# DeltaNet and low-rank mixer on one Trainium2 core: another order of the steps from the eighth chunk of the first recurrence on

## The chip, the cores and the metric

The kernel runs on one core of one Trainium2 chip. The metric is the device time of one execution in microseconds (us); of several executions the median is taken. Smaller is better.

## The reference

All data are float32. q, k and v have the shape (batch 4, heads 8, sequence 768, head size 48), beta (4, 8, 768). Two blocks follow each other:

```python
# 1. delta rule, for every batch and head a 48 x 48 state
k_n = k / (norm(k) + 1e-06)
for t in range(768):
    y[t] = q[t] @ state
    v_old = state.T @ k_n[t]
    state = state + beta[t] * outer(k_n[t], v[t] - v_old)
x = y.transpose(0, 2, 1, 3).reshape(4, 768, 384)      # heads side by side

# 2. low-rank mixer over the sequence, then a channel MLP
h = x.transpose(0, 2, 1) @ U @ V                       # U (768, 32), V (32, 768)
u = x + h.transpose(0, 2, 1)
out = u + relu(u @ w_ch1) @ w_ch2                      # (384, 1536), (1536, 384)
```

## The kernel before

**The recurrence in chunks.** A batch b is cut into two units, n = 2b and n = 2b + 1, each half of the sequence; a unit into six chunks of 64 tokens, so a batch has chunks 0 to 11. Within a chunk the tokens' dependence on one another is a triangular system, solved ahead of the recurrence; only the state of 48 x 48 goes from chunk to chunk. All eight heads are worked on together. The steps of a unit n, with their lines:

- load: q, k, v and beta come in by DMAs issued on SP and GpSimd.
- turn: k and q are transposed, in units 0 to 2 at least partly by TensorE (L681, copied out by ScalarE), in the others by VectorE (L756). i is 0 for k and 1 for q, j is the half of the heads.
- products: k k^T and q k^T of a chunk on TensorE (L709), copied out by ScalarE and VectorE (L740).
- norms: one operation on ScalarE and five on VectorE (L631 to L636), which give the scale of a token's key.
- blocks: VectorE lays the diagonal blocks for the substitution (L803), substitutes in many pairs of operations (L812, L818), and lays the result back (L825).
- joins, for half h of the chunks: small matmuls that put the blocks together (L869, L883, L909, L927), with copies on ScalarE and VectorE between them.
- prepare: two groups of matmuls that apply the solved system to k and v (L1032, L1043).

recur of batch b then goes chunk by chunk: state times key (TensorE, L1081), z = v minus that (VectorE, L1094), key times z (TensorE, L1109), new state (VectorE, L1120). outputs of chunk c multiplies q with the old state (L992) and adds the part within the chunk (L1006); ScalarE copies the result into X (L976). A TensorE group here has 16 matmuls.

**The mixer.** front of batch b and part i (256 tokens): for i = 0 the product with U (L1401), which VectorE copies (L1407); then the product with V (L1420), VectorE's addition (L1425), the transposes (L1444) and ScalarE's copy (L1447) into ut. channels e (0 to 5) is the first product of the MLP in two groups of six matmuls (L1505), with relu on ScalarE (L1470). add_up (L1532) and narrow e (L1625, gathered by VectorE at L1545) are the second product, written with seven products in place of eight for a 2 x 2 split. quick (L1305) is the first product of the last batch. load_weights turns the mixer's weights, which come in as 64-bit floats, into float32 on ScalarE (L1207) and VectorE (L1221, L1228, L1235), slice by slice; start i issues the DMAs of slice i (384 KB for most). reserve hands two of TensorE's result banks over to the MLP.

**Kinds of TensorE group.** L1401, L1444, L1505, L1625, L1305 and the turns use the array whole, or in column strips (L1401). The products, prepare, recur, outputs and L1420 use it as four quadrants of 64 x 64; the joins, as pieces of 32 x 32.

**What sets the order.** Every step above is a generator that yields one entry for each operation or small group it issues. The kernel waits for nothing at build time and plans nothing: a written table, ORDER, names for each of 2,259 positions the step that moves on by one. The order in which instructions are issued is the order in which each engine takes them from its queue; waits on other engines are put in as the data need them.

```python
ORDER = [x.rsplit(":", 1) for x in " ".join(ORDER.split()).split("; ")]
ORDER = {int(y): name for name, at in ORDER for y in at.split()}
...
def run():
    wake()
    for y in range(len(ORDER)):
        i = ORDER[y]
        s, got = waits[i], None
        ...
        advance(i, got, state["now"])
        wake()
```

An entry such as "outputs b0 c11: 467 473 478 480" says that the outputs of chunk 11 of batch 0 move on at those four positions (two TensorE groups, two ScalarE copies). Between the entries of one step those of other steps stand.

Of the kernel before, what the change touches and what calls it, by code (L numbers as in the profile page):

```python
# [27 lines left out]
def kernel(  # L28
# [116 lines left out]
    add_up b0 i0 f00: 615 655 660; add_up b0 i0 f03: 632 643 656; add_up b0 i1 f00: 794 798 818; add_up b0 i1  # L145
    f03: 826 827 829; add_up b0 i2 f00: 970 988 1025; add_up b0 i2 f03: 1018 1022 1032; add_up b1 i0 f00: 1164
    1193 1217; add_up b1 i0 f03: 1203 1206 1216; add_up b1 i1 f00: 1320 1332 1340; add_up b1 i1 f03: 1376 1382
    1395; add_up b1 i2 f00: 1522 1553 1593; add_up b1 i2 f03: 1566 1592 1596; add_up b2 i0 f00: 1678 1702 1728;
    add_up b2 i0 f03: 1718 1719 1727; add_up b2 i1 f00: 1873 1884 1890; add_up b2 i1 f03: 1878 1879 1893; add_up
    b2 i2 f00: 1994 2003 2018; add_up b2 i2 f03: 2038 2039 2044; add_up b3 i0 f00: 2177 2182 2183; add_up b3 i0  # L150
    f03: 2181 2184 2187; add_up b3 i1 f00: 2208 2209 2215; add_up b3 i1 f03: 2207 2214 2216; add_up b3 i2 f00:
    2225 2230 2241; add_up b3 i2 f03: 2226 2231 2232; blocks n0: 61 73 75 76 82 84 86 88 89 91 93 94 96 97 103
    110 114 122; blocks n1: 143 157 160 163 173 175 179 192 201 206 208 212 213 215 218 219 226 229; blocks n2:
    475 497 498 499 505 508 510 513 514 515 516 517 518 519 520 521 522 528; blocks n3: 687 699 700 704 716 727
    729 730 738 745 754 765 766 769 770 773 774 778 787 788 795 796 803 809 810 811 812 813 815 816 828 832 833
    835; blocks n4: 968 976 980 984 985 986 992 996 1002 1011 1026 1041 1053 1055 1057 1060 1062 1063 1075 1078
    1082 1104 1107 1109 1116 1117 1118 1119 1120 1121 1122 1130 1131 1132; blocks n5: 1161 1194 1226 1227 1228
    1231 1234 1239 1242 1243 1246 1254 1255 1257 1258 1266 1281 1285 1286 1289 1291 1300 1303 1310 1330 1333
    1334 1336 1337 1338 1339 1353 1365 1366; blocks n6: 1495 1507 1516 1518 1520 1521 1524 1526 1527 1528 1538
    1543 1544 1551 1555 1556 1580 1585 1590 1602 1603 1615 1616 1620 1640 1641 1646 1647 1653 1654 1665 1666  # L160
    1668 1669; blocks n7: 1673 1682 1683 1690 1691 1711 1745 1749 1750 1751 1760 1768 1769 1773 1776 1798 1804
    1805 1817 1818 1819 1820 1827 1828 1829 1830 1833 1834 1836 1837 1838 1839 1840 1844; both f0: 2127; both
    f1: 2097; both f2: 2163; both f3: 2123; both f4: 2151; both f5: 2179; channels b0 i0 e0: 523 524; channels
    b0 i0 e1: 525 531; channels b0 i0 e2: 532 543; channels b0 i0 e3: 553 555; channels b0 i0 e4: 573 574;
    channels b0 i0 e5: 595 624; channels b0 i1 e0: 748 760; channels b0 i1 e1: 761 764; channels b0 i1 e2: 771
    775; channels b0 i1 e3: 783 785; channels b0 i1 e4: 814 819; channels b0 i1 e5: 820 821; channels b0 i2 e0:
    898 899; channels b0 i2 e1: 907 908; channels b0 i2 e2: 932 933; channels b0 i2 e3: 957 966; channels b0 i2
    e4: 973 975; channels b0 i2 e5: 989 991; channels b1 i0 e0: 1114 1115; channels b1 i0 e1: 1125 1126;
    channels b1 i0 e2: 1128 1129; channels b1 i0 e3: 1138 1146; channels b1 i0 e4: 1153 1155; channels b1 i0 e5:
    1175 1181; channels b1 i1 e0: 1276 1277; channels b1 i1 e1: 1294 1295; channels b1 i1 e2: 1297 1298;  # L170
    channels b1 i1 e3: 1316 1321; channels b1 i1 e4: 1326 1356; channels b1 i1 e5: 1357 1359; channels b1 i2 e0:
    1449 1459; channels b1 i2 e1: 1477 1478; channels b1 i2 e2: 1499 1500; channels b1 i2 e3: 1509 1523;
    channels b1 i2 e4: 1529 1530; channels b1 i2 e5: 1540 1547; channels b2 i0 e0: 1642 1643; channels b2 i0 e1:
    1644 1645; channels b2 i0 e2: 1656 1657; channels b2 i0 e3: 1661 1663; channels b2 i0 e4: 1664 1679;
    channels b2 i0 e5: 1692 1693; channels b2 i1 e0: 1807 1809; channels b2 i1 e1: 1846 1847; channels b2 i1 e2:
    1849 1850; channels b2 i1 e3: 1852 1853; channels b2 i1 e4: 1857 1858; channels b2 i1 e5: 1862 1863;
    channels b2 i2 e0: 1946 1954; channels b2 i2 e1: 1957 1958; channels b2 i2 e2: 1959 1975; channels b2 i2 e3:
    1977 1987; channels b2 i2 e4: 1998 2008; channels b2 i2 e5: 2023 2032; copies f0: 2108 2116; copies f1: 2083
    2088; copies f2: 2144 2149; copies f3: 2091 2109; copies f4: 2102 2113; copies f5: 2147 2156; cut f0 k0 to0:
    2150; cut f0 k0 to1: 2148; cut f0 k1 to1: 2137; cut f1 k0 to0: 2138; cut f1 k0 to1: 2204; cut f1 k1 to1:  # L180
    2139; cut f2 k0 to0: 2166; cut f2 k0 to1: 2205; cut f2 k1 to1: 2203; cut f3 k0 to0: 2154; cut f3 k0 to1:
    2135; cut f3 k1 to1: 2172; cut f4 k0 to0: 2110; cut f4 k0 to1: 2188; cut f4 k1 to1: 2171; cut f5 k0 to0:
    2176; cut f5 k0 to1: 2202; cut f5 k1 to1: 2186; diagonals n0 h0: 188 190 191 195 210 222; diagonals n0 h1:
    167 169 171 176 181 186; diagonals n1 h0: 312 315 319 336 343 353; diagonals n1 h1: 290 292 303 338 349 358;
    diagonals n2 h0: 590 592 600 602 611 612; diagonals n2 h1: 649 650 678 680 681 691; diagonals n3 h0: 873 874
    875 878 895 897; diagonals n3 h1: 850 851 852 905 916 951; diagonals n4 h0: 1141 1142 1144 1145 1191 1209;
    diagonals n4 h1: 1170 1173 1184 1202 1207 1213; diagonals n5 h0: 1384 1390 1391 1420 1425 1428; diagonals n5
    h1: 1372 1378 1393 1407 1437 1438; diagonals n6 h0: 1695 1723 1734 1747 1765 1771; diagonals n6 h1: 1722
    1733 1735 1744 1753 1758; diagonals n7 h0: 1911 1912 1915 1919 1929 1940; diagonals n7 h1: 1891 1892 1935
    1936 1961 1963; first f0: 2132; first f1: 2101; first f2: 2157; first f3: 2125; first f4: 2104; first f5:  # L190
    2164; front b0 i0: 490 492 502 504 511 512; front b0 i1: 547 560 596 620; front b0 i2: 628 629 645 648;
    front b1 i0: 1061 1066 1070 1072 1096 1101; front b1 i1: 1113 1152 1250 1260; front b1 i2: 1307 1309 1410
    1431; front b2 i0: 1579 1589 1594 1614 1622 1630; front b2 i1: 1636 1726 1730 1777; front b2 i2: 1779 1783
    1854 1865; front b3 i0: 2035 2040 2042 2046 2048 2049; front b3 i1: 2057 2062 2063 2064; front b3 i2: 2067
    2070 2071 2072; gather b0 i0 h0 c0 finalFalse: 657; gather b0 i0 h0 c0 finalTrue: 668; gather b0 i0 h0 c1
    finalTrue: 740 918; gather b0 i0 h1 c0 finalFalse: 686; gather b0 i0 h1 c0 finalTrue: 741 884; gather b0 i0
    h1 c1 finalFalse: 693; gather b0 i0 h1 c1 finalTrue: 724; gather b0 i1 h0 c0 finalFalse: 830; gather b0 i1
    h0 c0 finalTrue: 834; gather b0 i1 h0 c1 finalTrue: 886 1133; gather b0 i1 h1 c0 finalFalse: 856; gather b0
    i1 h1 c0 finalTrue: 883 921; gather b0 i1 h1 c1 finalFalse: 868; gather b0 i1 h1 c1 finalTrue: 877; gather
    b0 i2 h0 c0 finalFalse: 1024; gather b0 i2 h0 c0 finalTrue: 1054; gather b0 i2 h0 c1 finalTrue: 1105 1178;  # L200
    gather b0 i2 h1 c0 finalFalse: 1071; gather b0 i2 h1 c0 finalTrue: 1110 1162; gather b0 i2 h1 c1 finalFalse:
    1068; gather b0 i2 h1 c1 finalTrue: 1079; gather b1 i0 h0 c0 finalFalse: 1204; gather b1 i0 h0 c0 finalTrue:
    1232; gather b1 i0 h0 c1 finalTrue: 1264 1871; gather b1 i0 h1 c0 finalFalse: 1244; gather b1 i0 h1 c0
    finalTrue: 1263 1504; gather b1 i0 h1 c1 finalFalse: 1248; gather b1 i0 h1 c1 finalTrue: 1249; gather b1 i1
    h0 c0 finalFalse: 1380; gather b1 i1 h0 c0 finalTrue: 1381; gather b1 i1 h0 c1 finalTrue: 1445 1739; gather
    b1 i1 h1 c0 finalFalse: 1400; gather b1 i1 h1 c0 finalTrue: 1436 1763; gather b1 i1 h1 c1 finalFalse: 1412;
    gather b1 i1 h1 c1 finalTrue: 1427; gather b1 i2 h0 c0 finalFalse: 1572; gather b1 i2 h0 c0 finalTrue: 1600;
    gather b1 i2 h0 c1 finalTrue: 1629 1785; gather b1 i2 h1 c0 finalFalse: 1607; gather b1 i2 h1 c0 finalTrue:
# [1495 lines left out]
```

## Time and profile before

| | before |
|---|---|
| median of 3 runs | 596.03 us (594.77 to 596.44) |
| the profiled execution's own time | 598.21 us |
| its span | 596.2 us |
| TensorE instructions | 10,428 matmuls, 10,428 weight loads |
| VectorE, ScalarE, GpSimd instructions | 1,011, 442, 229 |
| DMA, whole execution | 36.23 MB, mean 61 GB/s |
| mean granted TensorE clock | 0.943 |

The profile is of one execution, whose own time is 2.2 us above the median of the runs, and 2.0 us above its span. Engines are PE (TensorE matmuls), PEld (its weight loads, which overlap the matmuls), DVE (VectorE), ACT (ScalarE), POOL (GpSimd) and SP. "L1505" is line 1505 of the kernel. A view of stretches gives for each engine the busy us and, in brackets, the number of instructions, then the granted clock of TensorE as a share of full speed, the DMA engines' mean busy share and the rate. The chain of waits is followed back from the last instruction: each row is a start in us, a length, and what was running on it; "issue" is time in which an engine waited for nothing that the profile shows.

### The profile page before, as it was taken

The numbers are of one execution on the slowest core, as the hardware profiler recorded it, in microseconds if no ns is written. First come the engines' busy times: TensorE is split into PE (matmuls) and PEld (weight loads), VectorE is DVE, ScalarE is ACT, GpSimd is POOL, SyncE is SP. The second block draws the span as 40 slices with busy tenths as digits, with TensorE's granted clock in tenths as the row PEclk, the third lists the DMA queues.
The fourth block names the chain that finished last, engine by engine and source line by source line (L and its number), as shares of the span: only waits on it lengthen the run. The fifth ranks groups of instructions, "written<-read, shape, count | busy, mean of one in ns | idle before, by whom it ended". The sixth has DMA issues, their size and how long they took to land.

```text
span 596.2 us, 23454 instructions
## 1 busy us (share of the span) xinstructions
PE 557.4 (93%) x10428; PEld 481.2 (81%) x10428; DVE 409.6 (69%) x1011; ACT 216.5 (36%) x442; POOL 133.0 (22%) x229
## 2 busy tenths in 40 slices
PE   4778886899999999999999999999999999999997
PEld 3678775688989888789979888889898868656997
DVE  3888757999899459999777389888791134322532
ACT  2846473635421443045135421253225321234100
POOL 9122042056023603144006330082001000000000
PEclk9765565999999999999999999999999999999999
DMA  9971637724014511153003412331020000100001
GB/s 141 198 156 25 213 90 166 159 48 83 8 35 81 98 18 30 22 130 77 14 17 52 76 23 52 75 88 39 4 53 4 2 3 2 66 0 1 16 25 41
DMA packets 89445, 36.23 MB, mean 61 GB/s; under 512 B 75456, under 2 KB 87104, under 8 KB 89344
## 3 DMA queue, kind: packets, MB, share of 16 engines
q1 hardware_dynamic: 80800, 24.69, 20.2%
q0 software_dynamic: 6944, 9.74, 8.0%
q8 instruction: 82, 1.34, 1.0%
q10 hardware_dynamic: 1600, 0.30, 0.3%
q14 instruction: 19, 0.16, 0.1%
HBM read 29.98 MB, written 4.72 MB: 58 GB/s over the span
## 4 chain that ended last, share of the span: by engine, by line
PE 82%; DVE 10%; issue 3%; ACT 2%; DMA 1%; SPq 0%; DVEq 0%; ACTq 0%
PE P L1625 27%; PE P L1505 23%; PE P L1305 7%; PE P L709 4%; DVE xt L818 2%; DVE prod L812 2%; PE P L1081 2%; PE P L992 2%; PE P L1109 2%; PE P L1006 2%; PE P L883 2%; PE P L1043 2%; PE P L1032 2%; PE P L681 2%; PE P L869 2%
## 5 line engine op out<-in xcount | busy, mean ns | idle before, releaser
L1505 PE MATMUL P<-ut,w_sb 128*128 128x256 f32 x648 | 150.9, 385 | 0.9 <-ACT ut L1447 0.9
L1505 PEld LDWEIGHTS P<-ut,w_sb 128*128 128x128 f32 x648 | 119.7, 190 | 18.8 <-ACT ut L1447 1.1
L1625 PE MATMUL P<-w_sb,hs 128*128 128x192 f32 x540 | 95.5, 330 | 1.3 <-issue 1.2
L1625 PEld LDWEIGHTS P<-w_sb,hs 128*128 128x128 f32 x540 | 87.4, 190 | 5.4 <-issue 3.1
L818 DVE TENSOR_TENSOR xt<-xt,prod 128x112 f32<-128x112 f32 (+21 forms) x200 | 64.6, 323 | 6.9
L812 DVE TENSOR_TENSOR prod<-gs,xt 128x112 f32<-128x112 f32 (+21 forms) x200 | 63.4, 317 | 4.1
L1545 DVE TENSOR_TENSOR X<-X,P 128x192 f32<-128x192 f32 x84 | 29.0, 348 | 52.1 <-PE P L1625 52.0
L1470 ACT ACTIVATE hs<-P 128x512 f32<-128x512 f32 x54 | 32.1, 597 | 70.6 <-PE P L1505 63.1
L976 ACT COPY X<-P 64x192 f32<-64x192 f32 x96 | 30.0, 314 | 70.5 <-PE P L1006 64.0
L1625 PE MATMUL P<-w_sb,S 128*128 128x192 f32 x288 | 49.7, 328 | 0.0
L1625 PEld LDWEIGHTS P<-w_sb,S 128*128 128x128 f32 x288 | 46.7, 190 | 0.9 <-DVE X L1545 0.6
L550 POOL DMA_DIRECT2D slot<-in_k_dram x40 | 24.6, 622 | 45.6 <-DVE z L1094 21.2
L1094 DVE TENSOR_TENSOR z<-slot,P 128x192 f32<-128x192 f32 x44 | 15.5, 352 | 27.5 <-PE P L1081 26.3
L564 POOL DMA_DIRECT2D slot<-in_v_dram x32 | 21.1, 665 | 58.5 <-DVE slot L756 29.9
L948 ACT COPY slot<-zz 32x384 f32<-32x384 f32 x64 | 32.0, 508 | 5.4 <-DVE zz L825 2.5
L797 POOL MEMSET xt<- 128x1056 f32 x8 | 7.9, 985 | 115.4 <-DVE zz L825 115.3
L709 PE MATMUL P<-slot 48*64 48x64 f32 x1536 | 31.6, 234 | 1.3 <-DVE slot L740 0.7
L1305 PE MATMUL P<-slot,w_sb 128*128 128x384 f32 x96 | 32.8, 486 | 0.0
L709 PEld LDWEIGHTS P<-slot 48*64 48x64 f32 x1536 | 28.3, 147 | 5.0 <-issue 1.6
L1625 PE MATMUL P<-w_sb,slot 128*128 128x192 f32 x180 | 30.4, 327 | 0.9 <-DVE X L1545 0.9
L1120 DVE TENSOR_TENSOR s<-s,P 128x192 f32<-128x192 f32 x40 | 14.0, 350 | 25.1 <-PE P L1109 20.1
L564 POOL DMA_DIRECT2D slot<-in_k_dram x44 | 29.4, 670 | 8.0 <-PE P L1109 7.7
(153 smaller groups left out, 916.0 us busy)
## 6 DMA issues: line engine op xcount, KB each, us to landing
out_dram<-X SPq DMA_DIRECT2D x22, 192.0 KB, 2.2
w_sb<-in_moe_w_ch_dram SPq DMA_DIRECT2D x10, 384.0 KB, 5.7
slot<-in_k_dram SPq DMA_DIRECT2D x48, 72.0 KB, 3.3
slot<-in_k_dram POOLq DMA_DIRECT2D x44, 72.0 KB, 3.4
slot<-in_v_dram SPq DMA_DIRECT2D x32, 72.0 KB, 3.1
slot<-in_v_dram POOLq DMA_DIRECT2D x32, 72.0 KB, 3.0
X<-in_moe_w_ch_dram SPq DMA_DIRECT2D x6, 384.0 KB, 4.8
wide<-in_moe_w_ch_dram SPq DMA_DIRECT2D x6, 384.0 KB, 4.4
```

The lines of the kernel that those rows point to most:

```text
L550: queue.dma_start(out=blocked(n)[quarter(y % 4), j, g, :, 0:w], in_=src[b, 4 * g + 2 * j + par, hf * UC * L : (hf + 1) * UC * L, BK * low ...
L564: queue.dma_start(out=t[half(1 - g if name == "z" else g), :, to, 0:D], in_=src[b, 4 * g + s, hf * UC * L : (hf + 1) * UC * L, :].rearrang ...
L709: nc.tensor.matmul(p_g[half(g ^ (par * i)), par, c], kq[rows, c, j, 0, half(g)], kq[rows, c, j, i, half(g)], start=True, stop=True,)
L812: nc.vector.tensor_tensor(out=prod, in0=gb[:, :, j : j + 1, j + 1 :].to_broadcast([128, split, m, w]), in1=xb[:, :, 0:m, j : j + 1].to_bro ...
L818: nc.vector.tensor_tensor(out=xb[:, :, 0:m, j + 1 :], in0=xb[:, :, 0:m, j + 1 :], in1=prod, op=ALU.subtract,)
L948: nc.scalar.copy(pg[quarter(i), :, at, :, a : a + BK], cut(zc, h)[quarter(i)].rearrange("p r (c j) t -> p r c j t", j=2),)
L976: nc.scalar.copy(x[half(c % 2), c // 2, 4 * D * g : 4 * D * (g + 1)].rearrange("p (j r d) -> p r j d", r=2, d=D), states(p_y)[half(g)],)
L1305: nc.tensor.matmul(to, w, t, start=start, stop=stop, skip_group_check=True)
L1470: nc.scalar.activation(hs[:, fs[0] : fs[1] + 1 : fs[1] - fs[0]], p_f, ACTF.Relu)
L1505: nc.tensor.matmul(p_f[:, x], w(x, t), ut[:, t], start=(t == 0), stop=(t == KT - 1))
L1545: nc.vector.tensor_tensor(out=to, in0=to, in1=p, op=ALU.add)
L1625: nc.tensor.matmul(to, of[0], of[1], start=of[2], stop=of[3], skip_group_check=True)
```

## The change

Only the table changes. Each step keeps as many positions as before, positions 0 to 395 are the same, and from 396 (in chunk 7 of the recurrence of batch 0) on nearly all positions differ. No instruction is added or taken away, and no line number changes. A short part of the diff, with the entries side by side that matter most; the table has entries like these for all steps of all units:

```diff
-    recur b0: ... 378 387 398 399 401 402 404 406 410 411 420 421 426 434 462 463 468 472;
+    recur b0: ... 378 387 398 399 403 407 411 414 428 436 443 450 453 456 460 465 468 470;
-    outputs b0 c7: 391 409 416 417;        outputs b0 c10: 456 469 476 477;
+    outputs b0 c7: 391 405 406 426;        outputs b0 c10: 459 471 476 483;
-    outputs b0 c11: 467 473 478 480;       norms n2: 489 491 580 621;
+    outputs b0 c11: 467 479 484 485;       norms n2: 462 469 505 636;
-    turn n2 i0 j0: 436 440;                turn n2 i0 j1: 443;
+    turn n2 i0 j0: 420 422;                turn n2 i0 j1: 425;
-    products n2 i0 j0: 446 450 457 461 466;
+    products n2 i0 j0: 427 434 439 440 454;
-    products n2 i0 j1: 452 458 470 471 494;
+    products n2 i0 j1: 433 445 452 455 461;
-    blocks n2: 475 497 498 499 505 508 510 513 514 515 516 517 518 519 520 521 522 528;
+    blocks n2: 457 472 473 474 475 477 490 498 499 501 506 507 508 510 512 517 518 523;
-    joins n2 h0: 536 545 546 551 552 564 577 578 581 584 594 601 604 617 619 623;
+    joins n2 h0: 526 527 529 542 543 544 558 560 562 572 573 577 596 612 632 646;
-    load_weights: ... 379 392 400 405 407 412 429 435 441 442 453 454 455 479 539 554 561 568 586 599 606 616;
+    load_weights: ... 379 392 397 400 408 409 419 429 432 435 478 545 547 559 561 581 584 588 590 604 613 624;
-    load n2 k: 389 390 393 415 423 425 432 433;  start i10: 408 419;  start i11: 437 464;
+    load n2 k: 389 390 393 410 412 413 416 421;  start i10: 415 418;  start i11: 482 486;
-    reserve: 501;  front b0 i0: 490 492 502 504 511 512;  front b0 i1: 547 560 596 620;
+    reserve: 513;  front b0 i0: 492 493 496 500 502 504;  front b0 i1: 514 516 563 585;
-    channels b0 i0 e0: 523 524;            (the first L1505)
+    channels b0 i0 e0: 515 520;
-    recur b2: ... 1519 1525 1531 1537 1539 1545 1554 1558;   outputs b2 c11: 1548 1561 1562 1563;
+    recur b2: ... 1550 1553 1561 1562 1563 1566 1568;        outputs b2 c11: 1564 1572 1574 1575;
-    front b3 i0: 2035 2040 2042 2046 2048 2049;              narrow b2 i2 e0: 2036 2043;
+    front b3 i0: 2040 2041 2044 2046 2050 2051;              narrow b2 i2 e0: 2038 2049;
```

Read: in the old table the three last chunks of recur b0 (positions 420 to 472) have the turns and products of unit 2 behind or between them, and blocks n2 begins at 475, after recur's last position; in the new table the turns and products of unit 2 stand from 420 to 461, recur's last chunks from 428 to 470, blocks n2 begins at 457 and norms n2 at 462. Of load_weights twelve entries from 396 on stood ahead of the first L1505 at 523; nine do so ahead of 515 in the new table, eight of them ahead of 436. In front b3 i0 the table before has a group of narrow b2 i2 e0 (2036) between L1401 (2035) and L1420 (2042); in the new one that group is at 2038, ahead of both.

## The prediction

> **What bounds the kernel now.** The page first: the share of PE, its forty slices, the granted clock, and the queue that brings PE its instructions.
>
> ```profile
> span 596.2 us, 23454 instructions
> PE 557.4 (93%) x10428; PEld 481.2 (81%) x10428; DVE 409.6 (69%) x1011; ACT 216.5 (36%) x442; POOL 133.0 (22%) x229
> PE   4778886899999999999999999999999999999997
> PEclk9765565999999999999999999999999999999999
> q8 instruction: 82, 1.34, 1.0%
> ```
>
> PE is full from the eighth slice (some 118 us) to the end. Both programs hold the same 10,428 matmuls, so a new order can change only what lies between them: waits, changes of kind, clock. The stretch table says how much there is.
>
> ```profile
> core 0: us, PE busy (x) PEld busy (x) DVE busy (x) ACT busy (x) POOL busy (x), PEclk, DMA share, GB/s
> 92.30:99.10 6.80, 3.65 (x106) 3.06 (x104) 3.81 (x8) 1.57 (x5) 0.00 (x0) 0.50 0.98 195
> 99.10:102.50 3.40, 2.84 (x68) 2.54 (x69) 3.37 (x6) 1.81 (x4) 2.53 (x4) 0.50 0.43 132
> 102.50:105.90 3.40, 3.40 (x65) 3.07 (x66) 3.30 (x5) 1.91 (x3) 0.00 (x0) 0.50 0.13 18
> 105.90:117.70 11.80, 9.87 (x294) 6.71 (x289) 10.58 (x28) 7.66 (x15) 0.00 (x0) 1.00 0.83 189
> 117.70:508.20 390.50, 386.21 (x7439) 337.18 (x7440) 293.51 (x730) 133.85 (x274) 98.97 (x166) 1.00 0.22 44
> ```
>
> The change begins at step 396, at about 92 us. From there to 117.70 PE is busy 19.8 of 25.4 us, until 105.9 at half clock; from 117.70 to 508.20 it idles 4.3 us in all. From 508 on both orders run almost only big matmuls. So the opening and small things in the middle decide. The chain of waits, its opening window and three narrow windows, names them.
>
> ```profile
> 94.50 2.33 issue
> 101.69 2.82 PE P L681 x12
> 109.36 0.45 PE P L1006 x16
> 110.61 2.07 PE P L1401 x24
> ...
> 354.66 1.49 PE P L1505 x6
> 358.10 1.31 PE P L1505 x6
> 397.60 0.70 issue
> 418.01 0.35 issue
> 449.00 1.20 issue
> 487.32 2.07 PE P L1401 x24
> 489.39 2.15 PE P L1625 x12
> ```
>
> To see there: four stretches in which PE waits for no engine ("issue"); the same six matmuls of L1505 in 1.31 or 1.49 us, by what stands beside them; and in the last two rows a PE group (L1625) that covers the DVE copy (L1407) between L1401 and L1420.
>
> **Instruction blocks: -3.0 us.** 20,856 weight loads and matmuls over 82 packets of queue 8 are 254 a packet: instructions come in blocks of 256. Each "issue" row ends 1.4 to 1.5 us after such a packet has ended. By the packets' starts, a block's load begins when PE is some 57 instructions short of the block before it, and takes 3.4 to 3.6 us where the DMA engines are idle. So PE waits if it runs 313 instructions faster than that. Small groups do: 16 matmuls of L992, L1006 or L1081 in 0.23 us, 24 of L909 in 0.20 us. I laid the groups of each order end to end with their start-to-start times. After 117 us the old order has eight such stretches of 1.9 to 3.9 us of PE work; in the new one the shortest is 4.3 us. So the stops at 397.60, 418.01 and 449.00 go. They are 2.25 us as rows; by the start times the groups there take 0.9, 1.0 and 1.3 us longer than elsewhere. I take -3.0, ends -2.3 and -3.3. The stop at 94.50 stays: its block's load begins before step 396, in a stretch with the DMA engines 98% busy.
>
> The Trainium skill (Runtime: NRT & Kernel Launch, Instruction fetch mechanics) says that PE's instruction memory is refilled in 16 KiB blocks of 256 instructions while the current one runs, and that crossing a boundary is mostly hidden. The block size agrees with the 254; the rows of 2.33 and 1.20 us show that it isn't always hidden here. By the page this term would be zero.
>
> **Changes of kind: +0.7 us.** PE runs whole-array groups (L1505, L1625) and groups in quadrants or smaller. A whole-array group starts 1.295 us before the next one between its like, 1.39 before a change, 1.40 after one, 1.49 between two; L1006 takes 0.23 us before its like and 0.34 before a big group; a small group after a big one takes 0.04 more. A round trip costs 0.35 us. The old order enters whole-array work 71 times from another kind, the new one 73 times: 2 x 0.35.
>
> **New waits: +2.4 us.** Three are seen in the new order of PE against DVE.
> - In front b3 i0 the group L1625 that stood between L1401 and L1420 is now ahead of both. L1420 waits for the copy L1407 alone: 0.14 us to its start, 0.56 us, and restart; with the change of kind 0.9 us.
> - Late in recur b2 the state step of chunk 10 (L1109, then DVE L1120, 0.35 us) is followed at once by L992, which reads that state: 0.7 us, where a big group stood.
> - L869 of joins n2 h0 comes four big groups after L1505 begins, not nine, while the substitution of n2 is still on DVE: 0.6 us, and 0.3 us twice in its next two links.
>
> That is 2.8. One old wait goes: 0.4 us ahead of L1109 at 210.9. The half dozen waits of 0.24 us in each recurrence (z on DVE between L1081 and L1109) are about as many in both.
>
> **The opening: +0.4 us, ends -0.4 and +1.1.** Both stop until 96.8 us. Then the old order ends the recurrence up to chunk 9, and from 101.69 runs the turns and products of unit 2; the new one runs these first (two turns 2.8 us, products 1.5 and 1.45 us at half clock) and chunks 9 to 11 behind them. The work is the same, but not DVE's place in it: L803 (1.98 us) now stands ahead of the state of chunk 10, and the five operations of norms n2 (1.26 us) ahead of z of chunk 11; in the old order both came behind the last step. In exchange the conversions of weights (L1221, L1228, L1235: 2.6 us a slice) leave the recurrence: nine pieces from step 396 to the first L1505, not twelve. Step by step the last L1006 of chunk 11 comes at 110.8 instead of 109.4, and L1505 at 119.4 instead of 117.7, with 0.65 us of L1420 (front b0 i1) already done: +1.1 with the clock as it was. No cover is left for L803: each us more of DVE ahead of it is one more.
>
> The clock can give this back. It was granted at 105.9, after a stretch filled by turns and products; the small groups of 99.10 to 102.50 (2.84 of 3.40 us busy) had not been enough. The new order has turns and products from 97.8 on. If 99.1 to 102.5 suffices, PE's steps up to 105.9 take half: 1.4 us less, -0.4 net. I take the middle.
>
> The Trainium skill (TensorE: Matmul & The Clock Gate, What's actually happening) says that one busy window of about 3.4 us restores the full clock. By that rule the opening would be the -0.4 and the sum -0.3 us.
>
> DVE, ACT, POOL and SP keep their instructions. The loads of unit 2 are issued nearly as before (its fourth k piece ahead of a 384 KB weight transfer instead of behind it), and behind 117.7 us the DMA share is 0.22.
>
> **Sum.** -3.0 + 0.7 + 2.4 + 0.4 = +0.5 us: 598.7 against the profiled execution's own 598.21 (span 596.2), 2.2 above the median of the runs, 596.03. For that median: 596.5 us.
>
> **Rivals.**
> - *The blocks give nothing* (the page's rule above, or the stops come back elsewhere since a load takes longer than 4.3 us: the one at 94.50 took 8 us from its start, under DMA traffic). Then the sum is +3.5: 599.5. For it: DMA traffic is seen only in this one trace. Against: at a DMA share of 0.22 no load took over 4.3 us between its start and its use but one. 0.20.
> - *The turns of unit 2 wait for their data*, slower. They now stand ahead of chunk 9 in PE's queue, at 97.8 instead of 101.7 us. From 92.3 to 99.1 the DMA engines are 98% busy; k's pieces are issued from 85 to 90 us. Every us by which the last of them lands after 97.8 holds up the recurrence, up to the old place: 3.9 us, 600.4. Against: the pieces whose landing is shown came by 94 us. 0.08.
> - *The opening gains*, faster: the full clock a window earlier (-0.8 against my term) and the stop of 2.33 us shrinks, since its length hangs on what the DMA queues hold just then: 3.1 us less, 593.4. Against: the bytes asked for by 93 us are much the same. 0.14.
>
> The forecast has 0.50; 0.08 is left for waits that I haven't seen, which make it slower.
>
> **Numbers.** About 0.3% (1.8 us) is what a measurement of this kernel can tell from no change: 594.2 to 597.8 counts as the same. The forecast lies there, with all its ends; the blocks, the turns and the unseen waits lie above, the third rival below. Faster 0.14, same 0.50, slower 0.36. The range goes from 593.6 to 600.4: it holds the forecast's ends, the first rival, and about half of the rest.
>
> **What would show it.** Right: no "issue" row over 0.5 us after 117 us in the chain; the first L1505 between 117.9 and 119.5 us; L1401 and L1420 of front b3 i0 with some 0.8 us of idle PE between them; PE idle between the first L1505 and 508 us near 4.3 - 2.3 + 2.4 us. Wrong: "issue" rows of the old size at new places (first rival); L681 waiting for a DMA at 98 us (second); the first L1505 before 116 us (third); or an "idle before" of PE at a line not named here.

## The result and the profile after

The new table is slower: 600.45 us median of 22 runs (596.66 to 604.70) against 597.71 us (594.77 to 601.09) of 22 runs of the old one. The ratio is 1.0054, 95% interval 1.0033 to 1.0075, which is 2 to 4.5 us. The forecast was 596.5 us, range 593.6 to 600.4. A second comparison (new_again below) gave 1.0082 (1.0054 to 1.0110).

The two profiled executions don't show this: 598.21 us before, 598.28 after. That of the new table is the third fastest of its 22 runs. A single pair of traces misleads here, so what follows rests on several traces of each opening (the stretch from the first changed step to the first L1505).

The page of the profiled execution after: the span, the share of PE, its forty slices and the granted clock.

```profile
span 596.6 us, 23448 instructions
PE 558.9 (94%) x10428; PEld 479.8 (80%) x10428; DVE 410.2 (69%) x1011; ACT 214.8 (36%) x442; POOL 132.4 (22%) x229
PE   4787886999999999999999999999999999999997
PEclk9757558799999999999999999999999999999999
```

The stretch table, in the borders of before (for each engine the busy us, in brackets the instructions; then clock, DMA share, GB/s):

```profile
core 0: us, PE busy (x) PEld busy (x) DVE busy (x) ACT busy (x) POOL busy (x), PEclk, DMA share, GB/s
92.30:99.10 6.80, 5.67 (x159) 4.92 (x151) 6.19 (x10) 3.74 (x8) 0.00 (x0) 0.75 1.19 229
99.10:102.50 3.40, 2.34 (x128) 2.09 (x128) 2.30 (x8) 2.26 (x6) 2.57 (x5) 1.00 0.99 264
102.50:105.90 3.40, 2.20 (x26) 1.66 (x27) 2.95 (x7) 1.28 (x4) 3.25 (x6) 0.71 0.87 166
105.90:117.70 11.80, 10.47 (x215) 6.69 (x215) 8.78 (x30) 3.63 (x7) 3.28 (x5) 0.80 0.48 85
117.70:508.20 390.50, 386.10 (x7430) 335.65 (x7429) 292.77 (x720) 132.83 (x275) 90.55 (x153) 1.00 0.22 44
```

Behind 117.70 us PE idles 4.4 us in all, as forecast (4.3 - 2.3 + 2.4). The surprise is ahead of it: the full clock is back at 97.08 us, 9 us earlier than in the trace of before (105.97), and is lost again at 103.91.

The chain of waits, four windows of it (rows under 0.08 us left out):

```profile
89.06 6.76 DMA wide<-in_moe_w_ch_dram
95.93 0.09 ACT X L1207
96.02 0.72 issue
96.74 0.81 ACT slot L696
97.59 0.93 PE P L709 x48
...
102.68 1.20 issue
103.88 0.56 PE P L1109 x13
...
455.62 1.21 issue
456.82 0.37 DVE s L1120
...
488.98 2.12 PE P L1401 x24
491.12 0.57 DVE tt L1407
491.73 0.88 PE P L1420 x8
```

To see there: a weight transfer holds up L1207 on ScalarE, and behind it in the queue stand the copies (L696) that L709 waits for. There is a stop of 1.20 us ("issue") within L1109 of chunk 10, where the old table has none; the stop of 2.33 us that the trace of before has in chunk 8, at 94.50, is 0.60 us here. The old stops at 398, 418 and 450 us are gone; the "issue" row at 455.62 is DVE's, PE itself stood 0.34 us there. One stop of PE's of over 0.5 us is left behind 117 us: 0.64 us at 133.17, which new_again does not have. The wait of L1420 for L1407 in front b3 i0 is as forecast.

### The profile page after: what moved, and what is told of

It is laid out like the page before. It is cut to its first block, busy times and chain, and to the rows that moved or that the text cites. A ratio compares the mean times of both kernels' runs of the same rounds, so it can differ in the third digit from the quotient of the medians.

```text
span 596.6 us, 23448 instructions
## 1 busy us (share of the span) xinstructions
PE 558.9 (94%) x10428; PEld 479.8 (80%) x10428; DVE 410.2 (69%) x1011; ACT 214.8 (36%) x442; POOL 132.4 (22%) x229
## 4 chain that ended last, share of the span: by engine, by line
PE 85%; DVE 8%; DMA 2%; issue 2%; ACT 1%; SPq 1%; DVEq 0%; ACTq 0%
PE P L1625 28%; PE P L1505 24%; PE P L1305 7%; PE P L709 4%; PE P L1081 2%; PE P L883 2%; PE P L1109 2%; PE P L869 2%; PE P L992 2%; PE P L1032 2%; PE P L1006 2%; DVE xt L818 2%; PE P L1401 1%; PE P L1043 1%; DVE prod L812 1%
## 5 line engine op out<-in xcount | busy, mean ns | idle before, releaser
L1505 PE MATMUL P<-ut,w_sb 128*128 128x256 f32 x648 | 152.4, 386 | 0.1
L1505 PEld LDWEIGHTS P<-ut,w_sb 128*128 128x128 f32 x648 | 119.2, 190 | 18.2 <-ACT ut L1447 0.6
L1625 PE MATMUL P<-w_sb,hs 128*128 128x192 f32 x540 | 94.6, 329 | 0.0
L1625 PEld LDWEIGHTS P<-w_sb,hs 128*128 128x128 f32 x540 | 87.6, 190 | 2.6 <-issue 1.2
L1625 PE MATMUL P<-w_sb,S 128*128 128x192 f32 x288 | 50.1, 329 | 0.0
L1625 PEld LDWEIGHTS P<-w_sb,S 128*128 128x128 f32 x288 | 46.7, 190 | 2.7 <-issue 1.2
L955 POOL MEMSET slot<- 32x384 f32 x32 | 12.7, 411 | 99.8 <-PE P L912 70.0
L1305 PE MATMUL P<-slot,w_sb 128*128 128x384 f32 x96 | 33.1, 486 | 0.0
L709 PEld LDWEIGHTS P<-slot 48*64 48x64 f32 x1536 | 27.5, 142 | 6.5 <-issue 2.9
L709 PE MATMUL P<-slot 48*64 48x64 f32 x1536 | 30.9, 229 | 1.8 <-DVE slot L740 0.7
L1625 PE MATMUL P<-w_sb,slot 128*128 128x192 f32 x180 | 30.4, 327 | 0.9 <-DVE X L1545 0.9
L1625 PEld LDWEIGHTS P<-w_sb,slot 128*128 128x128 f32 x180 | 29.3, 190 | 1.8 <-DVE X L1545 1.5
```

The lines of the kernel that those rows point to most:

```text
L709: nc.tensor.matmul(p_g[half(g ^ (par * i)), par, c], kq[rows, c, j, 0, half(g)], kq[rows, c, j, i, half(g)], start=True, stop=True,)
L1305: nc.tensor.matmul(to, w, t, start=start, stop=stop, skip_group_check=True)
L1505: nc.tensor.matmul(p_f[:, x], w(x, t), ut[:, t], start=(t == 0), stop=(t == KT - 1))
L1625: nc.tensor.matmul(to, of[0], of[1], start=of[2], stop=of[3], skip_group_check=True)
```

## The experiments

Two theories run through the expectations. By the opening theory the loss lies between step 396 and the first L1505; by the middle theory it lies behind that. The block theory says that PE stops at borders between blocks of 256 of its instructions when a block has run too fast for the next to be there; such a stop is an "issue" row.

All openings are measured from the start of L1109 of chunk 7 (step 398, the first of recur behind step 396) to the first L1505; this leaves out what differs from run to run ahead of the change. "Half" is the time in it at half clock, "idle" the time in it that PE stood.

| trace | opening, us | half, us | idle, us |
|---|---|---|---|
| before; old_again | 25.71; 25.12 | 13.7; 10.2 | 5.65; 5.94 |
| old_then_new; old_then_new_late | 24.34; 24.38 | 6.8; 6.8 | 5.96; 5.74 |
| seam_late; old_stops | 24.58; 25.18 | 10.2; 10.2 | 5.07; 5.60 |
| **mean, old opening** | **24.9** | **9.7** | **5.7** |
| after; new_again | 26.77; 29.93 | 10.2; 17.1 | 5.82; 7.31 |
| new_then_old; new_then_old_late | 29.32; 26.47 | 13.7; 10.2 | 7.87; 6.29 |
| middle_filled | 30.49 | 17.0 | 8.78 |
| **mean, new opening** | **28.6** | **13.6** | **7.2** |

The new opening has done L1420 of front b0 i1 already (0.76 us from its start to L1505). So it is 28.6 - 24.9 - 0.8 = 2.9 us longer, about as much as the whole kernel. By the means of the traces 1.5 us of this is idle time, and 1.4 us is time in which PE was busy with the same matmuls for longer (21.4 less 0.8 us, against 19.2), for which the half clock is the one cause that the traces show. The idle time can be split further: "issue" stops make 3.4 us in the new opening and 1.8 in the old, all other waits together 3.9 and 3.8.

| kernel | ratio to before | 95% interval |
|---|---|---|
| old_again | 1.0004 | 0.9980 to 1.0028 |
| new_again | 1.0082 | 1.0054 to 1.0110 |
| new_then_old | 1.0124 | 1.0096 to 1.0153 |
| old_then_new | 1.0096 | 1.0066 to 1.0126 |
| old_then_new_late | 1.0041 | 1.0024 to 1.0059 |
| new_then_old_late | 1.0039 | 1.0013 to 1.0064 |
| seam_late | 1.0051 | 1.0032 to 1.0069 |
| act_later | 1.0021 | 0.9998 to 1.0045 |
| dve_later | 1.0070 | 1.0044 to 1.0096 |
| product_later | 1.0040 | 1.0017 to 1.0064 |
| opening_filled | 1.0035 | 1.0011 to 1.0059 |
| middle_filled | 1.0038 | 1.0012 to 1.0064 |
| all_filled | 1.0033 | 1.0011 to 1.0056 |
| new_act_middle | 1.0062 | 1.0040 to 1.0084 |
| spread2 | 1.0120 | 1.0092 to 1.0148 |
| new_pad64 | 1.0409 | 1.0359 to 1.0460 |
| old_pad64 | 1.0198 | 1.0174 to 1.0222 |
| old_stops | 0.9980 | 0.9963 to 0.9997 |

### Both tables again

No edit; the ratios are the first two rows of the table.

> The old table once more, for a second trace and for the spread of its executions. The clock is granted in windows of 3.41 us, and in the two profiles these windows begin at different places of the program (13.8 and 11.8 us). Opening theory: the time of an execution follows its granted clock, so this kernel's median is 597.7 us at a mean clock near 0.943, and its first L1505 comes at 117 to 119 us whatever the windows do. Middle theory: the same median; the spread is not tied to the clock.

> The new table once more. Its profiled execution (598.28 us) was one of the fastest of 22, with the clock at half in only two windows after 100 us. Opening theory: in most executions the new opening (PE idle while VectorE works L1425, L818 and L825 between 110 and 123 us) loses the full clock in one or two windows more: a mean clock near 0.936, a median of 600.5 us, and in a trace with a clock of 0.937 or less the extra half-speed windows lie between 97 and 130 us. Middle theory: clock as in the old table, and from the first L1505 to 508 us PE takes some 3 us longer than in the old table in every trace.

The new opening in the second trace took 29.93 us, with 17.1 us at half clock. From the first L1505 to L1305 the old table takes 390.36 and 390.98 us, the new one 390.96 and 390.53, with 0.76 us of work done before: 0.8 us more in the middle, not 3. The opening theory holds for its place, though not in all it said: the old table's first L1505 came at 116.44, ahead of its 117 to 119 us. The clock of a whole execution goes with its time only loosely (0.943 stands beside 595 and beside 600 us).

### Splices of the two tables

```diff
# steps in the order of the first table up to the cut, then all that is left in the order of the second
+ new_then_old:      new[0:523] + rest of old      old_then_new:      old[0:532] + rest of new
+ new_then_old_late: new[0:565] + rest of old      old_then_new_late: old[0:556] + rest of new
+ seam_late:         old[0:655] + rest of new, narrow b2 i2 e0 put behind L1401 of front b3 i0
```

> The new table up to the fourth group of L1505 (position 523), then every step that is left in the old table's order. Opening theory: +2 to +3 us against before, clock near 0.936. Middle theory: 0 +- 0.7 us, the old stops for instruction blocks near 398, 418 and 450 us being back.

> The old table up to the fourth group of L1505 (position 532), then every step that is left in the new table's order. Opening theory: between -1 and +0.7 us against before, clock near 0.943. Middle theory: +2 to +3 us.

> The old table up to the second group of channels b0 i0 e3 (position 555), then every step that is left in the new table's order: the first splice at the fourth L1505 left PE 4 us without work at 121 us, because the substitution of unit 2 was not yet done when the new table asked for its joins, and the clock fell there. Opening theory (the loss lies between step 396 and the first L1505): from -0.5 to +1.2 us against before, first L1505 at 115.4 to 117.7 us, no half-speed window after 107 us. Middle theory: +2.5 us or more, with full clock after 107 us.

> The new table up to the second group of channels b0 i0 e3 (position 564), then every step that is left in the old table's order: the counterpart of the old-then-new splice, which came out at 1.0041. Opening theory: the time from L1109 of chunk 7 to the first L1505 is 26.8 to 30 us, against 24.3 to 25.7 us in four traces with the old opening, and the whole is 2.5 to 4 us above before. Middle theory: at most 1 us above before.

> The old table up to the first step of recur b1 (position 654, behind the joins of unit 2), then every step that is left in the new table's order, with narrow b2 i2 e0 between L1401 and L1420 of front b3 i0. The earlier splice used up the L1505 groups ahead of the joins and so lost a clock window at 133 us; here the joins stand as in the old table. Opening theory: old opening and a middle without block stops: 0.5 to 1.5 us less than before, ratio 0.997 to 1.000. Middle theory: 1.003 or more.

Every splice is slower than the old table, whichever opening it has, so their totals settle nothing: the seam costs by itself. In old_then_new PE stood 3.3 us at 121.7 us, and three windows at half clock followed; the late splice lost one window at 133 us; seam_late lost none, and still needs 393.27 us from the first L1505 to L1305, against 390.4 to 391.0. Its ratio is the one that the middle theory asked for, but the time goes at the seam: from the first L1505 to that of channels b0 i2 e0 it takes 87.49 us, against 84.90 and 85.66 in the old table and 84.52 and 83.86 in the new. What they do give is the table of openings above, and one clean reading: from the first L1505 of channels b0 i2 e0 to L1401 of front b3 i0 the old order takes 284.65 and 284.51 us (before, old_again), the new order in seam_late 284.98. So between 204 and 489 us the two orders cost the same within 0.5 us, once narrow b2 i2 e0 stands between L1401 and L1420.

### Single steps of the new opening

```diff
-raised i10: 423        +raised i10: behind the last entry of products n2 i0 j1 (461)          # act_later
-blocks n2: 457, norms n2: 462 469    +all three behind the last entry of recur b0 (470)       # dve_later
-products n2 i0 j1: 433 +products n2 i0 j1: behind L1109 of chunk 9 (443)                      # product_later
```

> The new table with one ScalarE step moved: raised i10 (L1207) goes from ahead of the copies of unit 2's turns (L696) to behind the copies of its products. In both traces of the new table that L1207 waits for a 384 KB weight transfer (landed at 95.8 and 98.8 us), the copies stand behind it, and PE's L709 waits for them 0.5 and 1.5 us. If this wait counts: L709 follows its turns at once, 0.5 to 1.5 us less than the new table (599.0 to 600.0), more where it also saves a half-speed window. Rival (VectorE's queue sets the opening, as the prediction had it): no change against the new table, within 0.5 us.

> The new table with three steps of unit 2 moved behind the last step of the recurrence: L803 (1.98 us), the ScalarE operation of norms n2, and its five VectorE operations (1.26 us). VectorE theory (the prediction: each us ahead of the states of chunks 10 and 11 is one more): 1.5 to 3 us less than the new table. Opening theory (PE waits at that place for its next instruction block anyway, 0.9 to 2.3 us in the three traces with the new opening): within 0.5 us of the new table or slower, since the substitution starts later.

> The new table with one PE group moved: products n2 i0 j1 (L709, 48 matmuls, 0.88 us at full clock) goes from ahead of L992 of chunk 9 to behind L1109 of chunk 9, where PE now waits 0.55 us for the state (DVE L1120). If PE's idle time between 100 and 108 us is what loses the clock: the 0.55 us go, the following block stop stays, and the windows after 104 us are at full clock more often: 0.5 to 2 us less than the new table. Rival: what is saved is waited for at the block stop instead, 0 +- 0.3 us.

dve_later contradicts the prediction's cause: with L803 and the norms out of the way nothing is gained (opening 30.98 us). In the trace of after L803 ends at 104.17 us, while L1109, held by the block stop, ends at 104.44: DVE was not late. In dve_later that stop was 2.57 us. With raised i10 moved the wait of L709 is gone (opening 26.58 us, ratio 1.0021), but its interval (0.9998 to 1.0045) overlaps the new table's (1.0033 to 1.0075), and the stop in L1109 was 1.7 us long. product_later has a trace without a half-speed window behind 102.3 us (opening 26.67 us), the third fastest of its 12 runs; its ratio is 1.0040 (1.0017 to 1.0064), which does not part it from the new table.

### Filling the waits

```diff
# opening_filled: act_later and product_later, and
-turn n2 i1 j1: 489, its copy: 491   +behind L1401 of front b0 i0 (492)
-L1444 of front b0 i0: 502           +behind the group of products n2 i1 j0 (503)
# middle_filled
-narrow b2 i2 e0: 2038               +behind L1401 of front b3 i0 (2040)
-channels b0 i0 e2: 550              +ahead of the first L869 of joins n2 h0 (527)
# all_filled: both sets.   new_act_middle: act_later and middle_filled
```

> The new table with five steps of the opening moved so that PE has work where it waited: raised i10 behind the copies (as in the ScalarE experiment, 0.5 to 1.5 us), products n2 i0 j1 behind L1109 of chunk 9 (0.55 us), the turn n2 i1 j1 with its copy behind L1401 (0.76 us ahead of L1420), L1444 behind products n2 i1 j0 (0.45 us). Opening theory: the first L1505 comes 25 to 26 us after L1109 of chunk 7, with no half-speed window after 104 us, and the time is 2 to 3.5 us less than the new table, 0.998 to 1.002 of before. Rival (what is saved is waited for at the next instruction block): at most 1 us less than the new table, idle PE in the opening 6.5 us or more.

> The new table with two of the prediction's three new waits taken out: narrow b2 i2 e0 goes back between L1401 and L1420 of front b3 i0 (0.68 us in the trace, 0.9 in the prediction), and the first group of channels b0 i0 e2 goes ahead of L869 of joins n2 h0 (0.6 us). If the prediction's terms hold: 1.5 us less than the new table (ratio to before near 1.003), and the two idle times are gone from the trace. Rival: the waits only move, 0 +- 0.3 us.

> Both sets of moves in the new table. If opening and middle add up: 3.5 to 5 us less than the new table, ratio 0.995 to 0.999 to before, so faster than both tables. If the block stops take the opening's part back: 1.000 to 1.003.

> The new table with the ScalarE step of the opening moved (1.0021 alone) and the two middle waits filled. Opening 26.5 to 28.5 us by the granted clock. If the parts add up: 1 us less than with the ScalarE step alone, ratio 0.999 to 1.002. If the block stop and the clock in the opening decide: 1.002 to 1.004.

In opening_filled the rival came true. In it and in all_filled the four waits are gone, but two of 0.9 us came in their place (L992 behind ScalarE's copy L729, L1420 behind its copy L1447), and the stop in L1109 of chunk 10 has grown to 2.31 and 2.03 us, against 1.20 in after; openings 28.17 and 28.50 us, with two half-speed windows around and behind the stop. The middle waits are gone too (the first L1505 to L1305: 390.04 in middle_filled, 389.29 in all_filled, against 390.96 and 390.53), but 1 us doesn't show beside an opening that varies by 4 us: the ratio of middle_filled lies between theory and rival, that of all_filled just above the rival's. That of new_act_middle, 1.0062, lies above both. There a stop of 1.8 us stands at 134.42 us (0.4 us at the same place in middle_filled), and two half-speed windows followed.

### Where the clock is lost

In windows of 3.41 us that the clock itself has (same columns as the stretch table), after and then new_again:

```profile
97.08:100.50 3.42, 2.39 (x144) 2.26 (x147) 2.34 (x5) 2.56 (x6) 0.97 (x2) 1.00 1.02 261
100.50:103.91 3.41, 1.65 (x87) 1.28 (x78) 2.85 (x5) 2.07 (x3) 3.01 (x7) 1.00 1.08 266
103.91:107.32 3.41, 3.41 (x67) 2.88 (x66) 1.88 (x8) 0.88 (x3) 1.84 (x3) 0.50 0.53 94
107.32:110.74 3.42, 3.30 (x34) 2.06 (x34) 3.15 (x12) 2.83 (x6) 1.23 (x2) 0.50 0.34 44
```

```profile
101.21:104.62 3.41, 3.41 (x144) 3.41 (x140) 1.01 (x3) 1.96 (x5) 1.33 (x3) 0.50 0.97 259
104.62:108.03 3.41, 1.91 (x84) 1.49 (x77) 3.02 (x5) 1.75 (x3) 3.01 (x6) 1.00 0.66 160
108.03:111.45 3.42, 3.30 (x70) 2.77 (x69) 2.67 (x9) 1.48 (x5) 1.48 (x3) 0.50 0.25 55
```

For comparison, before, from where its full clock came back:

```profile
105.97:109.39 3.42, 2.46 (x136) 2.05 (x128) 2.71 (x8) 3.27 (x6) 0.00 (x0) 1.00 0.86 181
109.39:112.80 3.41, 3.41 (x48) 1.79 (x49) 3.27 (x8) 2.53 (x7) 0.00 (x0) 1.00 0.65 146
112.80:116.21 3.41, 3.33 (x112) 2.43 (x112) 3.21 (x11) 1.02 (x2) 0.00 (x0) 1.00 0.84 229
```

The window with the block stop has PE busy 1.65 and 1.91 us of 3.41, 48 and 56%, and the next two are at half clock. So in every trace of the new opening: 25 to 56% busy, then half. In the old opening no window behind its last half-speed one falls under 70%, and the clock stays. In the openings of act_later and product_later the lowest share was 60% and 65%, and it stayed as well.

All twenty traces say the same, counted from 84 us to the first L1505. Twenty-six windows at full clock had PE busy 56% or less, and the next window was at half after every one. Of seven windows with 59 to 61% five were followed by half, among them one of before, from 88.91 to 92.32 us with 60%. Behind fuller windows the clock stayed.

The Trainium skill (TensorE: Matmul & The Clock Gate, What's actually happening) lets the clock fall after an idle window and return after a busy one. Here it fell after windows half full, and in after it did not return behind 103.91 to 107.32, which was full. Up to L1305 it returned, in all traces, only behind windows with 90% and more (one with 81%), but not behind each of them: thirteen with 91 to 100% were followed by another at half.

### Spreading a turn

```diff
-turn n2 i0 j1: 425     +behind L1109 of chunk 9 (443)
-products n2 i0 j1: 433 +behind L1081 of chunk 10 (453), its copies behind it; raised i10 behind these
```

> The new table with one of unit 2's turns spread into the recurrence: turn n2 i0 j1 goes behind L1109 of chunk 9, its products behind L1081 of chunk 10 (and raised i10 behind both, as in the ScalarE experiment). The block of PE instructions whose successor comes late (4512 to 4768) holds in the new table only products and recurrence groups, in the old one two turns as well; here it holds one. Block theory: the stop in L1109 of chunk 10 (0.9 to 2.6 us in all traces of the new opening) shrinks by 0.7 us or more, the windows behind 103 us stay at full clock, first L1505 25 to 26.5 us after L1109 of chunk 7, ratio to before 0.999 to 1.003. Rival: the stop is as long as before, ratio 1.004 or more.

Neither came out whole. The stop in L1109 was gone (PE stood 0.9, 0.9 and 1.0 us for ScalarE's copies instead), yet the ratio is 1.0120: the clock stayed at half for 27.3 us, from 92.1 to 119.4, and the opening took 33.37 us. The products mixed with small groups left PE busy 1.3 to 2.7 us of each window until 109; the old order's two turns and two products in a row fill one (102.56 to 105.97 in before, 3.41 of 3.41) and bring the clock back.

### Moving the borders of the instruction blocks

```diff
     nc.vector.memset(P[:, :, 0:256], 0.0)
+    # on the same line, so that no line number changes:
+    [nc.tensor.matmul(P[quarter(i % 4), 0, 0:16], ident[quarter(i % 4), quarter(i % 4)],
+        ident[quarter(i % 4), 0:16], start=True, stop=True) for i in range(32)]
```

> The new table with 32 small matmuls (32 x 32 by 16 columns, 64 PE instructions, results not used) ahead of the first turn, where PE waits some 5 us for its first data. They move every border between instruction blocks 64 instructions forward in the program and change nothing else. Block theory: a border hurts where the 313 instructions ahead of it run in less than 3.55 us. From the trace of the new table that is nowhere behind the opening as it stands; moved by 64 it is at five places (near 133, 137, 204, 370 and 437 us), 7.4 us in all: from the first L1505 to L1305 5 to 8 us longer than in the new table, ratio to before 1.013 to 1.018. Rival (the page's rule, crossings are hidden): no change against the new table.

> The same 32 matmuls ahead of the old table. Block theory: the stop of 1.3 us at 450 us goes and no other of over 0.5 us comes behind 117 us, so from the first L1505 to L1305 1 us less than in the old table; what the moved borders do between 12 and 117 us can't be read from the traces, within 2 us either way. Rival: no change.

Sixty-four instructions more, run while PE waits for its first data, cost the old table 2.0% and the new one 3.5% (1.0409/1.0054). The chain of waits of the padded new table (an execution of 625.47 us; its six runs took 615.83 to 628.86), its issue rows between 117 and 440 us:

```profile
134.54 1.87 issue
147.35 2.03 issue
166.40 1.74 issue
222.91 1.69 issue
342.32 1.75 issue
428.22 1.36 issue
```

Three of the five places named are among them; the other three stops were not named, and two places named had none. The sum is 10.4 us. From the first L1505 to L1305 it took 409.03 us, 18.5 more than new_again: behind the first three stops the clock fell, for 17 us in all.

```profile
134.92:141.74 6.82, 5.33 (x61) 4.39 (x61) 4.59 (x8) 0.29 (x1) 0.00 (x0) 0.50 0.59 158
148.57:155.40 6.83, 6.02 (x53) 4.87 (x53) 5.47 (x11) 2.65 (x6) 0.00 (x0) 0.50 0.26 37
169.05:172.46 3.41, 3.41 (x13) 3.41 (x12) 0.67 (x1) 0.40 (x2) 0.00 (x0) 0.50 0.07 18
```

That these stops stand at borders can be counted. Number the matmuls in the order in which they start. In the twenty traces there are 118 stops of PE of 0.28 us and more behind 60 us for which the profile shows no releaser; divided by 128 (a matmul and its weight load are two instructions), their places leave 84 at 60 us, falling steadily to 58 at 450 us, and none lies elsewhere. The padded kernels follow the same count, so in them the borders stand 32 matmuls earlier in the table. In after the three stops of the opening are at matmuls 2130, 2255 and 2383.

So the mechanism is shown and its price was too low: a stop that empties half a window costs the window behind it as well. For the old table the forecast was wrong in sign (396.39 us for the same stretch, 5.7 more, with stops of 0.5 to 1.8 us at 140, 143, 148, 152 and 330): the limit of 313 instructions in 3.55 us doesn't name all stops.

### Three stops out of the old table

```diff
-narrow b2 i1 e2: 1921   +ahead of L1081 of chunk 7 of recur b3 (1917)
-channels b2 i1 e0: 1807 +ahead of prepare n6 h1's second group (1806)
-narrow b2 i0 e0: 1717   +ahead of the first L927 of joins n6 h0 (1712)
```

> The old table with three PE groups moved a few places, so that no block of 256 instructions holds small groups alone: narrow b2 i1 e2 ahead of L1081 of chunk 7 of recur b3 (it stood two groups later, behind the stop at 450 us), channels b2 i1 e0 ahead of the products that stop at 418 us, narrow b2 i0 e0 ahead of four groups of L927 with the stop at 398 us. The last two add a change of kind each (0.35 us). Block theory: the three stops (0.93, 1.0 and 1.2 us) go from the trace and 2 to 2.5 us from the stretch between the first L1505 and L1305 (390.4 and 391.0 us in the two traces of the old table): ratio 0.995 to 0.998. Rival (a stop only moves to the next border): ratio 0.999 to 1.001.

Ratio 0.9980, faster than both tables, 596.12 us against 597.06 in the same comparison. The chain at the places of the old stops:

```profile
394.67 0.51 ACT hs L1470
395.22 2.22 PE P L1625 x12
...
416.31 0.84 PE P L1043 x48
417.16 1.49 PE P L1505 x6
...
447.78 0.38 PE P L1081 x16
448.15 0.23 PE P L1006 x16
```

Among the 200 longest pieces of the chain no issue row is left behind 97 us. The stretch from the first L1505 to L1305 is 388.83 us, 1.5 and 2.1 us less than in the two old traces. In exchange PE now stands 0.97 us ahead of L1625 for the relu (the row of ACT at 394.67 is the end of that).

## Why the prediction was wrong

**The opening, +0.4 us, ends -0.4 and +1.1: the step that failed.** It measured +2.9. Three things in it:
- *The clock.* I asked only whether it comes back earlier. It did in the profiled run, at 97.08 us. I did not ask whether it is kept: the turns and products that bring it back were moved ahead of three chunks of small groups, whose windows are 25 to 56% busy. The table of openings has 13.6 us at half clock against 9.7; 4 us at half speed are up to 2 us of PE's work, and PE was busy 1.4 us longer. The working that gave -0.4 let the clock come back and had no step by which it could go again.
- *Instruction blocks.* I laid the blocks end to end only behind 117 us, and took the one stop at 94.50 as common. That it is, as a mean (the same border costs 1.5 to 2.3 us in the old opening and 0.6 to 3.1 in the new, 1.8 in both), but the next borders cost nothing in the old opening and 1.6 in the new. In the new opening PE's instructions 4512 to 4768 are one group of products, five of the recurrence and the start of a sixth; the old order has two turns and two products there. The stop in L1109 was 0.9 to 2.6 us long in four of the five traces of the new opening; in the fifth, new_then_old_late, PE had just stood 2.1 us ahead of L709. Idle PE is 7.2 us against 5.7, and these stops are the difference.
- *The queue of ScalarE.* raised i10, a step that I did not name, stands ahead of the copies of the turns and waits for a 384 KB transfer until 95.8 us (98.8 in new_again); L709 stood 0.5 and 1.5 us, and 2.1 in new_then_old_late, where the chain goes from such a transfer over VectorE's conversions to the copy. It is kin to the second rival, but the late data are weights, not k. As waits other than block stops are 3.9 us against 3.8 in sum, it only takes the place of waits that are gone, such as 0.89 us ahead of the first L1505.
- What I did name, L803 and the norms ahead of the last states, cost nothing in the trace of after: L803 runs there while PE stands at the block border.

**Instruction blocks behind 117 us, -3.0 us.** Right in kind: the three stops are gone from the new table's traces, and taking them out of the old table gave 1.5 to 2.1 us, after paying for two changes of kind (0.35 each, my estimate) and 0.97 for the relu; with these added back it is 3.2 to 3.8. But a new stop came, 0.64 us at 133.17 in after, where I had found no stretch under 4.3 us. The 3.4 to 3.6 us for a load are not in the packets either: at the three old stops the packet starts at 395.40, 416.06 and 447.83 us, 2.9, 2.3 and 2.4 us before PE goes on, and at 94.50 it starts at 93.74, 3.1 us before, not 8. The limit of 313 instructions is thus a fit that finds some of the stops. The first rival, that crossings cost nothing (the Trainium skill, Runtime: NRT & Kernel Launch, Instruction fetch mechanics, "mostly hidden"), is refuted by the padded tables. Its other half, stops at new places, came true in part: in the opening, and with the 0.64 us.

**Changes of kind and new waits, +0.7 and +2.4 us.** The waits are in the trace: 0.68 us ahead of L1420 in front b3 i0 (0.9 with the change of kind), 0.56 at L992 of chunk 11 of recur b2 (0.7), 0.63 ahead of L869 (0.6). The changes of kind were not tried by themselves. As a sum, blocks, changes and waits were to be +0.1 us; measured from the first L1505 to L1305, with the work done before, +0.8.

So the forecast was short by 2.5 us in the opening and 0.7 behind it. With its +0.5 that makes 3.7 us by the traces; the ratio says 3.2 (2 to 4.5). The rest up to 600.45 us is that the old table's own median is 597.71 us in 22 runs, not 596.03 in three.

**Open.** Why the block stop is there in most runs and not in all: the load of that block starts late (101.58 us in after, 1.1 us before PE stands), with a DMA share of 1.02 and 1.08 just then, but no run took the traffic away. The split of the 2.9 us into 1.5 us of stops and 1.4 us of clock is read from the traces; no run took away one and left the other as it was, and none brought the new opening back to the old one's time: of act_later the interval overlaps that of the new table, filled waits came back as a longer stop, and spread2 lost the stop and the clock with it.

## What to carry to other kernels

A gap in PE's work costs its own length and, when it empties about half of one of the clock's windows, part of the next windows too; so ask of a new order where the clock is kept, not only where it returns. Lay the blocks of 256 PE instructions over the whole order, the opening above all: in this kernel each wants a group of large matmuls in it, and one edit ahead moves all borders behind it (64 instructions cost 2 to 3.5% here). Where time varies by 1% from run to run, compare several traces from a common step, not one pair.

## What was not expected of the hardware

The time of this program hangs on the count of its instructions: 64 more of them, run in idle time, made the old table 12 us longer (609.04 against 596.90) and the new one some 21 (3.5%). Up to the first L1505 the full clock went after every window with PE 56% busy or less and after none with 62% and more; among small groups of 32 x 32 behind 117 us it also went after 78 and 81% (old_then_new_late, act_later), and it stayed after one window of 54% (new_then_old_late, 449.53 us), so the share of busy time is not all that it goes by.
